# Turning the row maxima of an attention kernel with products in PV's form, and sending them in eight pieces

## The chip, the core and the metric

One core of a Trainium2 chip runs the whole program. Its engines work side by side, each from a queue of its own: TensorE (PE; its weight loads are PEld), VectorE (DVE), ScalarE (ACT), GpSimd (POOL) and SyncE (SP, which here issues nearly all DMAs). The metric is the device time of one execution in microseconds. The comparison is of medians of several runs.

## What is computed

An adaLN block: layer norm with shift and scale, attention with 32 query heads and one key and value head, a second layer norm, a bilinear GLU. The change touches the attention, more exactly the maximum that its softmax takes off the scores.

```python
S, D, H = 2048, 512, 32              # Dh = D // H = 16, F = 1792
h = layernorm(x) * (1 + ca) + sa     # sa, ca, ga, sb, cb, gb from silu(c) @ w_mod
q = (h @ wq) by heads; k = h @ wk; v = h @ wv     # one k and v for all heads
scores = einsum("bhqd,bkd->bhqk", q, k) * Dh ** -0.5
p = softmax(scores)                  # over 2048 keys
x = x + ga * (einsum("bhqk,bkd->bhqd", p, v) by heads @ wo)
h = layernorm(x) * (1 + cb) + sb
x = x + gb * (((h @ w_gate) * (h @ w_up)) @ w_down)
```

## The kernel before, in words

The attention is cut into 32 units of 256 queries and 8 heads. A unit has 16 steps over blocks of 128 keys. The scores are made twice. A first pass (`max_mm`, line 601) makes them with queries on the partitions, and VectorE takes the maximum of each row of 512 keys (line 605). A second pass (`qk_exp`, lines 657 and 659) makes them with keys on the partitions, ScalarE takes their exponential into a tile P (line 661), and `pv` (line 670) multiplies P by V. The first pass runs ahead of the second by LEAD steps, so that the maxima of unit u + 1 are complete some six steps before the second pass comes to it.

The maximum reaches the second pass as two more rows of its contraction. The query tile `sst[u % 3]` has 48 rows per half with the query in split f16, and rows 48 and 49 of each half (partitions 48, 49, 112 and 113) with the maximum divided by 32, split in two f16 parts; the key tile `kst` has -32 in the same rows. That is why the first pass reads 48 rows and the second 50. The maxima lie on 128 partitions by 16 columns (queries by blocks), and have to be turned before they can lie along a row. `max_fin` (line 622) takes the last maximum; `max_rows` gives back two functions: `f` turns the maxima on TensorE, and `g` splits them on ScalarE (line 634, the high part) and VectorE (line 635, the rest) and has SP send both to the rows of `sst` (line 639).

The code is written in the order in which each engine is to run it (`manual_schedule`); there is no scheduler behind it. `max_half` puts `f` and `g` aside for the next step. `late_max` calls `f` from `end_turn`, as a rule right behind `pv`, and `g` goes to `posts`, which are issued at the next opportunity. One unit's `pv` works in four products at a time, each of 32 columns of V, into four blocks of 32 partitions. Products of 64 rows in two halves (line 511, the projections and the GLU, and lines 601 and 659) stand around it.

In the first units SP also brings slices of the GLU weights into `hfs`, f32 slots in the tile `kwb`, for GpSimd to square and sum over rows (lines 944 and 946) into `ssqs`, which lie in the same tile: slots 4 to 7.5 and 8 to 11.5. The slots that the slices use are named in `SLOTS` (line 35). `kng`, half a slot behind slot 11, is read by the first unit's first pass alone.

Of the kernel before, what the change touches and what calls it, by code (L numbers as in the profile page):

```python
# [13 lines left out]
F32 = mybir.dt.float32  # L14
F16 = mybir.dt.float16
# [7 lines left out]
BT = S // NB  # L23
# [8 lines left out]
SQ_GAP = 2.6  # L32
LAG = 2
ROW_LAG = 4
SLOTS = (0, 1, 2, 3, 6, 7)
SUM_GAP = 4.0
SUM_LAG = 3
SPLIT_GAP = 2.5
# [25 lines left out]
def adaln_mqa_glu_kernel(ctx: ExitStack, tc: tile.TileContext, x_in, wq_in, wk_in, wv_in, wo_in,  # L64
                         wg_in, wu_in, wd_in, c_in, wm_in, out):
    nc = tc.nc
# [3 lines left out]
    consts = ctx.enter_context(tc.tile_pool(name="consts", bufs=1))  # L70
    big = ctx.enter_context(tc.tile_pool(name="big", bufs=1))
    work = ctx.enter_context(tc.tile_pool(name="work", bufs=2))
# [7 lines left out]
    def ps_hold(name="side", shape=(128, 512)):  # L80

        tag, bufs = pool.popleft()
        t = psum.tile(list(shape), F32, name=name, tag=tag, bufs=bufs)
        held[id(t)] = (t, tag, bufs)
        return t

    def ps_give(t):
        _, tag, bufs = held.pop(id(t))
        pool.append((tag, bufs))
# [47 lines left out]
    ident = consts.tile([128, 128], F32, name="ident")  # L137
# [8 lines left out]
    for i in range(3):  # L146
        t = consts.tile([128, 2, 2, ST], F16, name=f"sst{i}")
# [76 lines left out]
    kwb = big.tile([128, 2 * FT * D], F16, name="kwb", tag="wd")  # L224
    hfs = kwb[:, 0:2 * NHF * BT].bitcast(F32).rearrange("p (n t) -> p n t", n=NHF)
    ssqs = [kwb[:, 2 * n * BT:2 * n * BT + 2 * F].bitcast(F32) for n in (KC, 2 * KC)]
    kng = kwb[:, 2 * NHF * BT:2 * NHF * BT + BT]

    def hf(b, k):
# [107 lines left out]
    for k in range(KC):  # L337
        for j in range(4):
            nc.tensor.matmul(pmA[32 * j:32 * j + 32, 0:256], silr[:, k, 0:32], wmA[:, k, 256 * j:256 * j + 256],
                             start=(k == 0), stop=(k == KC - 1))  # L340
# [275 lines left out]
        relus.clear()  # L616

    mms = {}

    def max_fin(u):  # L620
        mms[u] = work.tile([128, 2, 8], F32, name="mm")
        nc.vector.tensor_reduce(mms[u], mparts[u], axis=AX.X, op=OP.max)

    def max_rows(u):
        def f():
            mms[u, "b"] = ps_hold("mxt")
            p = mms[u, "b"][0:16, 0:128]
            mms[u, "p"] = p
            nc.tensor.transpose(p, mms[u].rearrange("p a c -> p (a c)"), ident)  # L629

        def g():
            p = mms[u, "p"]
            mt = [work.tile([16, 128], F16, name=f"mt{hl}") for hl in range(2)]
            nc.scalar.activation(mt[0], p, AF.Copy, scale=1.0 / 32.0)
            nc.vector.scalar_tensor_tensor(mt[1], p, 1.0 / 32.0, mt[0], op0=OP.mult, op1=OP.subtract)
            ps_give(mms[u, "b"])
            s = sst[u % 3]
            for hl in range(2):
                nc.sync.dma_start(s[48 + hl:113 + hl:64].rearrange("p c q n -> p (c q n)"), mt[hl])
        return [(100, f, g)]  # L640

    pvb = {}
# [250 lines left out]
    def late_weights():  # L893
# [35 lines left out]
        taken = [0]  # L929

        def stage(n):
            if "d" in W:
                t = work.tile([128, D], F32, name="wsl", tag="xl", bufs=3)
            else:
                t = hfs[:, SLOTS[taken[0] % len(SLOTS)], :]
                taken[0] += 1
            nc.sync.dma_start(t[:, :sl[n][3]], sl[n][2])
            st[n] = t
# [24 lines left out]
        def norms(order):  # L963
            ns = [n for m in order for n in range(len(sl)) if sl[n][0] == m]
            out = []
            waiting = deque()
            for j in range(len(ns) + LAG):
                q = j - LAG

                def f(j=j, q=q):  # L970
                    if j < len(ns):
                        stage(ns[j])
                    if q >= 0:
                        square(ns[q])
                out.append((SQ_GAP, nothing, f))
                if waiting and j >= waiting[0][0]:
                    out.append((0,) + sums(*waiting.popleft()[1:]))
                if q >= 0 and (q == len(ns) - 1 or sl[ns[q]][0] != sl[ns[q + 1]][0]):
                    waiting.extend((j + SUM_LAG, sl[ns[q]][0], n) for n in range(4))
            out.append((SUM_GAP, nothing, nothing))  # L980
            return out + [(2,) + sums(*w[1:]) for w in waiting]

        def row_norms(ns):
            out = []
            for j in range(len(ns) + ROW_LAG):
                def f(j=j):
                    if j < len(ns):
                        stage(ns[j])
                    if j >= ROW_LAG:
                        t, n = st[ns[j - ROW_LAG]], j - ROW_LAG  # L990
                        nc.scalar.activation(t, t, AF.Square, accum_out=rown[:, n:n + 1])
                out.append((0, nothing, f))
            return out
# [66 lines left out]
        def split(n):  # L1060
            m, (i, c), v, w = sl[n]

            def load():
                if m < 2 and "g" not in W:
                    W["g"] = big.tile([128, 2, KC, F], F16, name="wg", tag="wg")
                    W["u"] = big.tile([128, 2, KC, F], F16, name="wu", tag="wu")
                elif m == 2 and i == 0:
                    W["d"] = big.tile([128, 2, FT, D], F16, name="wd", tag="wd")
                stage(n)

            def gate():
                if m >= 2:
                    nc.gpsimd.tensor_tensor(st[n], st[n], gbb if m == 2 else gab, op=OP.mult)

            def halves():
                t = st[n][:, :w]
                wt = wo if m == 3 else W["gud"[m]]
                if m < 2:
                    nc.gpsimd.tensor_scalar(t, t, sca[:, m:m + 1], 0.0, op0=OP.mult, op1=OP.add)
                nc.gpsimd.tensor_scalar(wt[:, 0, i, c], t, 1.0, 0.0, op0=OP.mult, op1=OP.add)  # L1080
                nc.gpsimd.tensor_tensor(wt[:, 1, i, c], t, wt[:, 0, i, c], op=OP.subtract)
            return load, gate, halves
# [45 lines left out]
    def max_half(a):  # L1128
        n = mstep[a]
        mstep[a] += 1  # L1130
        if n >= len(flat):
            return
        u, i, last, ops = flat[n]
        max_parts(u)
        for kind, p, t, kc in ops[a]:
            max_mm(u, a, (kind, p, t, kc))
        if mstep[1 - a] <= n:
            return
        u, i, last, ops = flat[n]
        if 0 < u < NU - 1 and i == QPRE:  # L1140
            load_q(u + 1)
        if i == 12:
            max_parts(u + 1)
        if last:
            max_fin(u)
            (_, f, g), = max_rows(u)
            later[min(mstep) + 1] = (f, g)
# [164 lines left out]
    u = NU - 1  # L1312
# [64 lines left out]
```

## Time and profile before

| | us |
|---|---|
| median of 3 runs | 1664.51 (1664.37 to 1664.66) |
| the profiled execution: span | 1663.8 |
| TensorE busy | 1643.3 (99%) |
| VectorE busy | 1402.3 (84%) |
| ScalarE busy | 1234.8 (74%) |
| GpSimd busy | 523.5 (31%) |
| TensorE's share of the chain that ended last | 93% |

The profile is of one execution. An engine's busy time is a union of its instructions; TensorE's products overlap in the records, so that the distance between their starts tells what one costs, not its duration. A row of the timeline joins instructions of the same kind that follow one another (x8 is eight), with the start in us from the beginning of the span, and behind it the duration of the whole. A q behind an engine's name (SPq, PEldq) is its sequencer, which waits and issues.

### The profile page before, as it was taken

Reading aid. Unit: us, or ns where it says so; the run is one execution under the profiler, and the core shown is the slowest. Engines: PE = TensorE matmul, PEld = TensorE weight load, DVE = VectorE, ACT = ScalarE, POOL = GpSimd, SP = SyncE. Lnnn points to the kernel's source line nnn. Section 1 sums busy time; section 2 is a strip of 40 time slices with the busy share of each in tenths; the row PEclk is TensorE's granted clock in tenths of the full one; section 3 lists DMA queues with packets and bytes.
Section 4 is the critical chain, followed back from the end, with each engine's and each line's share of the span. In section 5 each row is a group of like instructions: output and inputs, shape, how many; then the busy total and the mean of one; then the engine's idle time right before and its main releaser. Section 6 shows DMA issues by size and latency. Waiting matters only on the chain.

```text
span 1663.8 us, 39821 instructions
## 1 busy us (share of the span) xinstructions
PE 1643.3 (99%) x15677; PEld 747.1 (45%) x15677; DVE 1402.3 (84%) x2434; ACT 1234.8 (74%) x2389; POOL 523.5 (31%) x833
## 2 busy tenths in 40 slices
PE   8899999999999999999999999999999999999999
PEld 4333333355533554335543355434545345454776
DVE  7999999998998999899998999999998999980211
ACT  5688888888777877777877787777878777877300
POOL 4857537864841111301112011300113001210322
PEclk9999999999999999999999999999999999999999
DMA  6313313342210001000000000000000000000100
GB/s 237 108 59 100 95 43 120 96 129 80 77 51 24 18 12 32 19 32 20 20 26 23 25 13 24 26 25 26 20 29 15 26 22 20 26 14 21 33 13 14
DMA packets 66024, 75.39 MB, mean 45 GB/s; under 512 B 17702, under 2 KB 46634, under 8 KB 65836
## 3 DMA queue, kind: packets, MB, share of 16 engines
q1 hardware_dynamic: 63724, 72.26, 13.7%
q8 instruction: 123, 2.02, 0.5%
q10 hardware_dynamic: 2112, 0.59, 0.1%
q14 instruction: 65, 0.53, 0.1%
HBM read 55.51 MB, written 17.04 MB: 44 GB/s over the span
## 4 chain that ended last, share of the span: by engine, by line
PE 93%; ACT 2%; DVE 2%; DMA 1%; issue 1%; POOL 0%; SPq 0%; ACTq 0%; DVEq 0%
PE side L511 41%; PE pv L670 30%; PE mx L601 8%; PE sc L659 8%; PE sc L657 3%; ACT P L661 2%; DVE mpart L605 1%; DMA xbig<-in_A_x_dram 1%; PE mx L805 1%; PE mxt L629 0%; ACT hf L813 0%; PE sc L601 0%; DVE bs L248 0%; DMA kwb<-in_B_w_down_dram 0%; DMA wkv<-in_A_wv_dram 0%
## 5 line engine op out<-in xcount | busy, mean ns | idle before, releaser
L605 DVE TENSOR_REDUCE mpart<-mx 128x1 f32<-128x512 f32 x2016 | 1274.1, 684 | 104.0 <-PE mx L601 95.7
L661 ACT ACTIVATE P<-sc 128x512 f32<-128x512 f32 x2048 | 1094.8, 598 | 274.2 <-PE sc L659 226.9
L601 PE MATMUL mx<-kst,sst 48*128 48x512 f16 x2032 | 631.5, 377 | 3.8 <-ACT P L661 1.7
L659 PE MATMUL sc<-sst,kst 50*128 50x512 f16 x1792 | 597.5, 379 | 0.6 <-ACT P L661 0.3
L670 PE MATMUL pv<-P,vst 128*32 128x512 f32 x4096 | 545.3, 605 | 0.7
L511 PE MATMUL side<-h2T,wg 64*128 64x256 f16 (+1 forms) x2396 | 540.8, 271 | 0.1
L511 PE MATMUL side<-h2T,wu 64*128 64x256 f16 (+1 forms) x2396 | 538.7, 270 | 0.0
L511 PEld LDWEIGHTS <-wg 64*128 64x128 f16 (+1 forms) x2396 | 226.0, 94 | 230.5 <-ACT P L661 194.0
L511 PE MATMUL side<-wd,glu 64*128 64x512 f16 (+1 forms) x1172 | 272.8, 378 | 0.2 <-ACT P L661 0.2
L850 POOL TENSOR_SCALAR glu<-gf 128x256 f16<-128x256 f32 x112 | 45.8, 409 | 671.3 <-DVE gf L849 583.9
L511 PEld LDWEIGHTS <-wu 64*128 64x128 f16 (+1 forms) x2396 | 226.4, 94 | 43.0 <-issue 7.8
L601 PEld LDWEIGHTS <-sst 48*128 48x128 f16 x2064 | 189.9, 94 | 34.2 <-issue 17.4
L659 PEld LDWEIGHTS <-kst 50*128 50x128 f16 x1792 | 162.9, 94 | 63.0 <-issue 50.3
L511 PEld LDWEIGHTS <-glu 64*128 64x128 f16 (+1 forms) x1172 | 98.5, 94 | 192.4 <-ACT P L661 85.9
L670 PEld LDWEIGHTS pv<-P,vst 128*32 128x32 f32 x4096 | 80.7, 108 | 160.9 <-issue 150.1
L849 DVE TENSOR_TENSOR gf<-side,g 128x256 f32<-128x256 f32 x112 | 46.7, 418 | 79.8 <-ACT g L847 77.7
L657 PE MATMUL sc<-sst,kst 50*128 50x256 f16 x512 | 96.9, 268 | 0.1
L511 PE MATMUL side<-h,wq 64*128 64x512 f16 (+1 forms) x372 | 95.0, 376 | 0.4 <-ACT P L661 0.4
L847 ACT ACTIVATE g<-side 128x256 f32<-128x256 f32 x112 | 42.3, 379 | 65.6 <-PE side L511 65.3
L511 PE MATMUL side<-wo,och 64*128 64x512 f16 (+1 forms) x360 | 86.3, 377 | 0.0
L851 POOL TENSOR_TENSOR glu<-gf,glu 128x256 f16<-128x256 f32 x112 | 75.3, 673 | 9.3
L706 POOL TENSOR_TENSOR oc<-oc,rr 128x256 f32<-128x256 f32 x31 | 22.7, 731 | 146.6 <-DMA rr<-ri 100.4
(233 smaller groups left out, 865.4 us busy)
## 6 DMA issues: line engine op xcount, KB each, us to landing
pd<-ev SPq DMA_DIRECT2D x32, 256.0 KB
kwb<-in_B_w_gate_dram SPq DMA_DIRECT2D x32, 224.0 KB
kwb<-in_B_w_up_dram SPq DMA_DIRECT2D x32, 224.0 KB
sst<-qd SPq DMA_DIRECT2D x180, 32.0 KB
qd<-q SPq DMA_DIRECT2D x16, 256.0 KB
oc<-pd SPq DMA_DIRECT2D x64, 64.0 KB
rr<-ri SPq DMA_DIRECT2D x64, 64.0 KB
x<-in_A_x_dram SPq DMA_DIRECT2D x14, 256.0 KB
```

Of the source, the lines that this page charges most:

```text
L511: return nc.tensor.matmul(self.p[:, c * w:(c + 1) * w], left[rows], right[rows], start=start and c == 0, stop=stop and c == len(terms) - 1)
L601: nc.tensor.matmul(m, s[64 * a:64 * a + 48, t // 2, p, t % 2 * 128:(t % 2 + 1) * 128], w[64 * a:64 * a + 48, :], start=(i == 0), stop=(i = ...
L605: nc.vector.tensor_reduce(part, m, axis=AX.X, op=OP.max)
L657: nc.tensor.matmul(t[:, c * ST:(c + 1) * ST], keys, s[64 * a:64 * a + 50, c, p, :], start=True, stop=True)
L659: nc.tensor.matmul(t.rearrange("k (c n) -> k c n", c=2), keys, s[64 * a:64 * a + 50, :, p, :], start=True, stop=True)
L661: ex = nc.scalar.activation(ptl[u, kt, p, a], t, AF.Exp)
L670: nc.tensor.matmul(pvb[u][32 * j:32 * j + 32, :], vst[:, kt, :], ptl[u, kt, p, a], start=(kt == 0), stop=(kt == KT - 1))
L706: eng.tensor_tensor(o, o, st["r"], op=OP.mult)
L847: nc.scalar.activation(g, p[:, 0:ST], AF.Copy, scale=2.0 ** -45)
L849: nc.vector.tensor_tensor(gf, p[:, ST:2 * ST], g, op=OP.mult)
L850: nc.gpsimd.tensor_scalar(glu()[:, 0, f, :], gf, 1.0, 0.0, op0=OP.mult, op1=OP.add)
L851: nc.gpsimd.tensor_tensor(glu()[:, 1, f, :], gf, glu()[:, 0, f, :], op=OP.subtract)
```

## The change

The maxima go to a fixed tile `mmc`, 32 columns wide for each of two units in turn, of which 16 are used and 16 stay zero. Instead of one transpose of 128x16, `f` makes four f32 products whose stationary operand is this 128x32 tile and whose moving operand is a block of 32 columns of the identity; each goes to 32 partitions of PSUM of its own, as the four products of `pv` do. The turned maxima then lie on 128 partitions by 32 columns (16 of every 32 partitions count) instead of 16 by 128, and each of the two f16 parts goes to `sst` in four transfers, each from sixteen rows. The last two slots of the weight slices move from 6 and 7 to 12 and 13, behind the squares.

```diff
-SLOTS = (0, 1, 2, 3, 6, 7)
+SLOTS = (0, 1, 2, 3, 12, 13)
...
+    stg = kwb.bitcast(F32).rearrange("p (n t) -> p n t", t=BT)
...
+    mmc = consts.tile([128, 2, 32], F32, name="mmc")
+    nc.gpsimd.memset(mmc, 0.0)
 
     def max_fin(u):
-        mms[u] = work.tile([128, 2, 8], F32, name="mm")
+        mms[u] = mmc[:, u % 2, 0:16].rearrange("p (a c) -> p a c", a=2)
         nc.vector.tensor_reduce(mms[u], mparts[u], axis=AX.X, op=OP.max)
 
     def max_rows(u):
         def f():
             mms[u, "b"] = ps_hold("mxt")
-            p = mms[u, "b"][0:16, 0:128]
+            p = mms[u, "b"][:, 0:32]
             mms[u, "p"] = p
-            nc.tensor.transpose(p, mms[u].rearrange("p a c -> p (a c)"), ident)
+            for j in range(4):
+                nc.tensor.matmul(p[32 * j:32 * j + 32, :], mmc[:, u % 2], ident[:, 32 * j:32 * j + 32], start=True, stop=True)
 
         def g():
             p = mms[u, "p"]
-            mt = [work.tile([16, 128], F16, name=f"mt{hl}") for hl in range(2)]
+            mt = [work.tile([128, 32], F16, name=f"mt{hl}") for hl in range(2)]
...
             for hl in range(2):
-                nc.sync.dma_start(s[48 + hl:113 + hl:64].rearrange("p c q n -> p (c q n)"), mt[hl])
+                to = s[48 + hl:113 + hl:64].rearrange("p c q (h j n) -> p j (c q h) n", h=2, j=4)
+                for j in range(4):
+                    nc.sync.dma_start(to[:, j], mt[hl][32 * j:32 * j + 16, :])
...
-                t = hfs[:, SLOTS[taken[0] % len(SLOTS)], :]
+                t = stg[:, SLOTS[taken[0] % len(SLOTS)], :]
```

In the program the change shows on three queues. On TensorE near the end of unit 5, where the maxima of unit 6 are turned; before (line 670 is PV, 511 a side product of the GLU, 659 the scores):

```order
2907 L670 MATMUL pv<-P,vst 32x512 x3
2908 L670 MATMUL pv<-P,vst 32x512 [waits Activation_49]
2909 L629 MATMUL mxt<-ident,mm 16x128 [waits DVE_49,PE_49]
2910 L511 LDWEIGHTS wg [waits Activation_49]
2911 L511 MATMUL side<-h2T,wg 128x256 [waits Pool_49]
```

The same place in the changed program, where the lines count six more:

```order
2911 L676 MATMUL pv<-P,vst 32x512 x3
2912 L676 MATMUL pv<-P,vst 32x512 [waits Activation_49]
2913 L633 MATMUL mxt<-ident,mmc 32x32 [waits DVE_49,PE_49]
2914 L633 MATMUL mxt<-ident,mmc 32x32 x3
2915 L512 LDWEIGHTS wg [waits Activation_49]
2916 L512 MATMUL side<-h2T,wg 128x256 [waits Pool_49]
```

Four products stand where the transpose stood, with its waits and its neighbours. On SP, where the rows are sent behind that (mt is the split maximum, DMAHW names the eight counters that DMAs are waited for by); before:

```order
182 L937 DMA kwb<-in_B_w_gate_dram 128x448 [waits DMAHW2_49,Pool_49]
183 L639 DMA sst_128<-mt_5130 2x8x128 [waits DMAHW3_49,Activation_49]
184 L639 DMA sst_128<-mt_5131 2x8x128 [waits DMAHW4_49,DVE_49]
185 L937 DMA kwb<-in_B_w_gate_dram 128x448 [waits DMAHW5_49,Pool_49]
186 L937 DMA kwb<-in_B_w_down_dram 128x512 [waits DMAHW6_49,Pool_49]
```

And in the changed program:

```order
219 L645 DMA sst_128<-mt_5182 2x8x32 [waits DMAHW7_49,Activation_49]
220 L645 DMA sst_128<-mt_5182 2x8x32 [waits DMAHW0_49]
221 L645 DMA sst_128<-mt_5182 2x8x32 [waits DMAHW1_49]
222 L645 DMA sst_128<-mt_5182 2x8x32 [waits DMAHW2_49]
223 L645 DMA sst_128<-mt_5183 2x8x32 [waits DMAHW3_49,DVE_49]
224 L645 DMA sst_128<-mt_5183 2x8x32 [waits DMAHW4_49]
225 L645 DMA sst_128<-mt_5183 2x8x32 [waits DMAHW5_49]
226 L645 DMA sst_128<-mt_5183 2x8x32 [waits DMAHW6_49]
227 L943 DMA kwb<-in_B_w_gate_dram 128x448 [waits DMAHW7_49,Pool_49]
228 L943 DMA kwb<-in_B_w_down_dram 128x512 [waits DMAHW0_49,Pool_49]
```

Eight transfers stand in the place of two, the weight slices behind them, and the eight take all eight counters. On TensorE where unit 6 begins and its first scores read the rows; before:

```order
2993 L670 MATMUL pv<-P,vst 32x512 x4
2994 L511 LDWEIGHTS wg [waits Activation_49]
2995 L511 MATMUL side<-h2T,wg 128x256
2996 L659 LDWEIGHTS kst [waits DMAHW4_49,DMAHW3_49]
2997 L659 MATMUL sc<-sst_128,kst 128x512 [waits PE_49]
```

And in the changed program:

```order
2998 L676 MATMUL pv<-P,vst 32x512 x4
2999 L512 LDWEIGHTS wg [waits Activation_49]
3000 L512 MATMUL side<-h2T,wg 128x256
3001 L665 LDWEIGHTS kst [waits DMAHW4_49,DMAHW5_49,DMAHW3_49,DMAHW6_49,DMAHW2_49,DMAHW7_49,DMAHW1_49,DMAHW0_49]
3002 L665 MATMUL sc<-sst_128,kst 128x512 [waits PE_49]
```

The order is the same; the weight load of the first scores waits for all eight counters instead of two.

## Rows read from the trace of the kernel before

**Rows 1.** The page: span, TensorE's busy time, the chain that ended last.

```profile
span 1663.8 us, 39821 instructions
PE 1643.3 (99%) x15677; PEld 747.1 (45%) x15677; DVE 1402.3 (84%) x2434; ACT 1234.8 (74%) x2389; POOL 523.5 (31%) x833
...
PE 93%; ACT 2%; DVE 2%; DMA 1%; issue 1%; POOL 0%; SPq 0%; ACTq 0%; DVEq 0%
```

**Rows 2.** Busy time by stretch; then who VectorE's maxima (line 605) wait for, 500:1500.

```profile
core 0: us, PE busy (x) PEld busy (x) DVE busy (x) ACT busy (x) POOL busy (x), PEclk, DMA share, GB/s
...
500.00:1000.00 500.00, 499.48 (x5061) 227.51 (x5059) 457.93 (x770) 393.51 (x754) 83.15 (x149) 1.00 0.07 22
1000.00:1500.00 500.00, 499.26 (x5073) 227.84 (x5069) 457.07 (x770) 393.24 (x755) 87.20 (x161) 1.00 0.07 22
...
  PE mx L601: 76.1, 229
```

**Rows 3.** Timeline of TensorE, end of unit 5: start, duration, engine, line, operation, count.

```profile
327.51 1.06 PE L670 MATMUL pv<-P,vst 128*32 128x512 f32 x8
328.51 0.28 PE L629 MATMUL mxt<-ident,mm 128*16 128x128 f32 x1
328.72 0.28 PE L511 MATMUL side<-h2T,wg 64*128 64x256 f16 x1
```

**Rows 4.** Timeline of TensorE in unit 0, products of line 956 behind PV.

```profile
112.57 1.06 PE L670 MATMUL pv<-P,vst 128*32 128x512 f32 x8
113.45 0.40 PE L956 MATMUL mx<-kwb,onec 128*32 128x128 f32 x8
113.78 0.39 PE L659 MATMUL sc<-sst,kst 50*128 50x512 f16 x1
```

**Rows 5.** Timeline of SP, rows for units 2, 6 and 14; a pair in unit 16.

```profile
154.81 1.20 SPq L639 DMA_DIRECT2D sst<-mt  x2
...
329.11 1.19 SPq L639 DMA_DIRECT2D sst<-mt  x2
...
707.62 1.19 SPq L639 DMA_DIRECT2D sst<-mt  x2
...
824.72 1.10 SPq L700 DMA_DIRECT2D rr<-ri  x2
```

**Rows 6.** Issues by line: ns min/median/max; then six of line 566 in the timeline.

```profile
L639 SPq DMA_DIRECT2D sst<-mt x64: 508/542/659, 68.9 to 1500.8; - x64
...
L700 SPq DMA_DIRECT2D rr<-ri x64: 507/526/545, 137.6 to 1563.1; - x64
...
825.91 2.75 SPq L566 DMA_DIRECT2D sst<-qd  x6
```

**Rows 7.** Timeline of SP, from the rows for unit 30 on.

```profile
1453.92 1.19 SPq L639 DMA_DIRECT2D sst<-mt  x2
1465.70 0.34 SPq L679 DMA_DIRECT2D pd<-ev  x1
1467.71 0.57 SPq L686 DMA_DIRECT2D rc<-pd  x1
1468.38 1.09 SPq L690 DMA_DIRECT2D oc<-pd  x2
1478.19 0.34 SPq L695 DMA_DIRECT2D ri<-rc  x1
1479.94 1.09 SPq L700 DMA_DIRECT2D rr<-ri  x2
```

**Rows 8.** Busy time and DMA share (last but one) behind the issues at 1453.92.

```profile
1455.10:1455.20 0.10, 0.10 (x6) 0.05 (x2) 0.10 (x1) 0.10 (x1) 0.00 (x0) 1.00 0.14 33
...
1455.30:1455.70 0.40, 0.40 (x8) 0.16 (x8) 0.40 (x2) 0.37 (x2) 0.00 (x0) 1.00 0.00 0
...
1455.80:1455.95 0.15, 0.15 (x8) 0.00 (x0) 0.15 (x1) 0.15 (x1) 0.00 (x0) 1.00 0.09 19
1455.95:1456.20 0.25, 0.25 (x8) 0.00 (x0) 0.25 (x2) 0.25 (x2) 0.00 (x0) 1.00 0.00 0
```

**Rows 9.** Timeline of TensorE's weight loads: first scores of units 2, 6 and 14.

```profile
159.54 0.09 PEld L659 LDWEIGHTS <-kst 50*128 50x128 f16 x1 [0.84 <-issue]
...
334.46 0.09 PEld L659 LDWEIGHTS <-kst 50*128 50x128 f16 x1
...
712.11 0.09 PEld L659 LDWEIGHTS <-kst 50*128 50x128 f16 x1
```

**Rows 10.** Timeline of ScalarE behind the transpose for unit 6.

```profile
328.82 0.27 ACT L634 ACTIVATE mt<-mxt 16x128 f16<-16x128 f32 x1 [0.54 <-PE mxt L629]
329.20 2.12 ACT L661 ACTIVATE P<-sc 128x512 f32<-128x512 f32 x4
```

**Rows 11.** TensorE's second wait ahead of the transpose: ns min/median/max.

```profile
L629 PEldq EVENT_SEMAPHORE  x31: 51/51/51, 68.2 to 1452.4; - x31
```

**Rows 12.** Timeline: a weight load that waited for ScalarE's P.

```profile
331.55 0.09 PEld L511 LDWEIGHTS <-wg 64*128 64x128 f16 x1 [0.84 <-ACT P L661]
```

**Rows 13.** TensorE's waits for GpSimd's squares: us in total, times, longest.

```profile
PE mx L956 <- POOL kwb L946: 1.6, 1, 1.6
```

## The prediction

> **What bounds the kernel now.** I read the page first [rows 1]: TensorE is busy for 99% of a span of 1663.8 us, and 93% of the chain that ended last is its own. Then the stretches [rows 2]: from 500 to 1500 us it has under 1.5 us of idle time in 1000, at full granted clock, while VectorE is busy for 915 us and ScalarE for 787. So in the 32 units whatever shortens TensorE's stream shortens the kernel, and whatever stops that stream is added in full: nothing behind it could win the time back. The reader should see in the rows of VectorE's waits that its maxima still wait for TensorE 229 times in this stretch [rows 2]; it is close to full, but it follows.
>
> The path that the change touches is one per unit: the transpose of the maxima on TensorE, two short splits on ScalarE and VectorE, transfers issued by SP, and then the first score product of the next unit, which needs the rows that they bring. It is short work, so I looked at two distances: what the transpose holds of TensorE, and how long before their use the rows arrive.
>
> **What the turning costs.** For unit 6, at the end of unit 5, two sets of four P times V products start at 327.51, the transpose at 328.51, the next products at 328.72 [rows 3]: 1.21 us from the first PV product to the next work. The products of the form that the new ones copy are in the kernel already: line 956, 128x32 in f32, behind the same two sets. There they begin 0.88 us after the first PV product, and two sets of 128 columns hold the engine for 0.33 us until the next work [rows 4]. So staying in PV's form saves 0.12 us ahead of the products (1.00 against 0.88), and the switch is then paid once, behind them. Two sets of 512 columns took 0.88 us, 0.44 each; in proportion a set of 128 takes 0.11, and of the 0.33 us for two such sets and the switch 0.11 is left for the switch. One set of 32 columns is then 0.03 us, with the switch 0.14, with 0.02 for issuing four products instead of one 0.16: the new way takes 0.88 + 0.16 = 1.04 us against 1.21. I take 0.16 us saved; the ends are 0 (the one set costs as much as both sets there) and 0.22 (only the switch remains). Over 32 units that is 5.1 us of gain (0 to 7).
>
> **What the sending costs.** SP issued two transfers per unit, and 1.19 us were enough for both. Eight now stand in a row in its queue, one behind the other. The price of an issue: two of line 639 take 1.19 us, each with two waits; pairs with one wait take 1.09 and 1.10 us (lines 690 and 700) [rows 5 to 7]. The cheapest issues are those of line 566, six in 2.75 us, 0.47 a step [rows 6]. The new transfers have the shape of the old ones with shorter runs (two partitions by eight runs, out of sixteen partitions), so I take the dear kind: six steps of 0.57 (1.10 less line 700's median issue of 0.53) and one of 0.66, where the first transfer of the second half has two waits. The eighth issue begins 6 x 0.57 + 0.66 = 4.08 us after the first; the ends are 3.3 (0.47 a step) and 4.6 (0.66 a step).
>
> From the beginning of an issue to its landing no row gives the SBUF-to-SBUF time directly. In unit 30 the packets of the two transfers move 1.2 to 1.3 and 1.8 to 2.0 us after the first issue, so the second's data are there 1.3 us after its own beginning [rows 7, 8]; waiters are released 1.75 us after the issue of ri and 2.01 us after that of pd [rows 7], which both go to DRAM. I take 1.65, with ends 1.3 and 2.0. Last landing: 4.08 + 1.65 = 5.73 us after the first issue, where it was 0.66 + 1.65 = 2.31.
>
> The first score product of the next unit loads its weights at 334.46 in unit 6, 5.35 us after the first issue at 329.11 [rows 5, 9]. Up to now the rows were there some 3 us ahead, and nobody waited. Both ends of this distance move. The turning ends earlier: 0.12 us for the start, the rest from shorter splits (ScalarE's took 0.27 us over 128 columns [rows 10], now 32); I take 0.20 for the first issue, ends 0.10 and 0.26. The product becomes due earlier too, by the 0.16 us saved: 5.19 us after the old first issue.
>
> The weights load also has a new set of waits: eight DMA queues instead of two. A second wait costs TensorE's sequencer a 51 ns instruction of its own [rows 11], and the queues are waited for in a fixed order, whichever landed last; by the program's order some three remain behind the last landing on average, 0.15 us. From the end of a wait to the load it released I take 0.23 us: ScalarE's P tiles end at 331.32, the load that waited for them starts at 331.55 [rows 10, 12].
>
> So the load can start at 5.73 + 0.15 + 0.23 - 0.20 = 5.91 us, and is due at 5.19: TensorE stands for **0.72 us**. I count 25 units like unit 6. In units 1 to 3 the product comes earlier, in unit 2 4.73 us after the first issue [rows 5, 9]; with that for all three each loses 1.34 us, 4.0 together. In unit 14 it comes after 4.49 us [rows 5, 9], which gives 1.6. In units 0, 4 and 10 other work stands before it, it comes after the rows, and nothing is lost. Sum: 25 x 0.72 + 4.0 + 1.6 = 23.6 us lost, 5.1 gained, 18.5 to the worse.
>
> By the Trainium skill, "DMA: Bandwidth & Descriptors", Issuing engines are not separate DMA queues, the time that a sequencer takes to initiate a DMA is usually small beside the DMA itself. Here the issue of line 639 has a median of 0.54 us [rows 6], a third of the way to the landing, so the rows speak against it; if it held for the new transfers, the sum would be the gain alone, the time of the first rival below.
>
> **The rest costs nothing that I can price.** The two splits get shorter and stay hidden: ScalarE waited 0.54 us for the transpose [rows 10]. Their extra waits, for transfers of two units before, are passed in that idle time. The maxima now lie in one fixed tile, used in turn by even and odd units, which is as deep as the two buffers before; its clearing is one GpSimd instruction at the start. SP's other transfers behind the eight start 3.4 us later: weight slices in the first units and rows of x later, which are asked for several steps ahead; if that cover were gone, GpSimd's weight work and then TensorE would wait. Of the new slots, two weight slices no longer land on columns of the accumulated squares. That takes a wait away from SP and GpSimd, neither of which is on the path; the only place where TensorE waits for the squares is one of 1.6 us [rows 13], so at best 1.6 us is gained. I count 0.
>
> **Rivals.** *The rows come in time and only the gain is left.* If an issue costs what line 566's costs, the eighth begins at 3.3 + 0.05 us and lands at 3.35 + 1.65 = 5.0, or 4.8 with the earlier start, and the load could go at 5.03: ahead of 5.19. Then the whole gain stays: 1664.5 - 5 = 1659.5, faster. For it: SP has done six in 2.75 us. Against it: those have another shape, and the shape that is kept never took under 0.51 us.
>
> *The rows come in time, but the waits are in the way.* Six more waits of 51 ns stand on TensorE's sequencer right ahead of the load, 0.31 us, of which the end of the PV products covers some. 0.15 to 0.2 us a unit eats the 5.1 us: 1660 to 1667, no change.
>
> *The whole queue is slow.* If each issue takes 0.66 us or the landing 2.0, a unit loses 0.4 to 0.5 us more: 1693 to 1699 (29 units), and with both some 1709.
>
> *The change doesn't do what it says:* the small products switch the array's form after all. Then the 5.1 us are missing, and the forecast's mechanism gives 1688.
>
> **How the numbers follow.** The profiled execution's span is 0.7 us under the median of the runs, 1664.5; I add the difference to the median: 1664.5 + 18.5 = 1683.0. Chances: the wait for the late rows, in the sizes from 1668 to 1702, 0.70 (with the case without the gain in it); slower still 0.06; waits in the way of rows that are in time 0.14; the gain alone 0.10. A difference of 0.2%, 3.3 us, is about what can be told from no change here: faster 0.10, same 0.14, slower 0.76. The range leaves out the slowest case and the pure gain: 1660 to 1700.
>
> **What would show it.** In the profile after: the first score product of a unit, or the side product beside it, waits for a DMA (the tile sst from mt) in some 29 units, 0.5 to 1.3 us each; TensorE's idle time in the stretch from 500 to 1500 us rises from 1.3 to some 17 us; eight issues stand in a row in SP's timeline and take 4.6 us; from the first PV product to the work behind the turned maxima 1.05 us instead of 1.21. I am wrong if that row of issues takes under 4 us, if the data land in under 1.3 us, or if the products behind PV don't start at 0.88 us.

## The result and the profile after

The changed kernel takes 1671.72 us (median; 1670.99 to 1672.88) against 1664.59 for the one before: a ratio of 1.004, 95% interval 1.0028 to 1.0051. It is slower by 7.1 us, not by the forecast 18.5. One of its six executions took 3600 us, for a reason that no run here shows: the range and the ratio leave it out, and without it the median is 1671.47.

The page of the changed kernel: span, busy time, the chain that ended last, and the score products of line 665 (busy us, mean ns of one | idle time ahead of them, and what ended most of it); last, from the view of the waits, how long those products waited for the transfers of the rows (us in total, times, longest).

```profile
span 1669.7 us, 40589 instructions
...
PE 1644.7 (99%) x15901; PEld 756.8 (45%) x15901; DVE 1397.8 (84%) x2434; ACT 1232.3 (74%) x2389; POOL 525.1 (31%) x834
...
PE 89%; DVE 5%; ACT 3%; DMA 1%; issue 1%; SPq 1%; POOL 0%; ACTq 0%; DVEq 0%
...
L665 PE MATMUL sc<-sst,kst 50*128 50x512 f16 x1792 | 597.1, 378 | 6.7 <-DMA sst<-mt 4.2
...
PE sc L665 <- DMA sst<-mt: 4.2, 6, 0.8
```

Against [rows 1] the span is 5.9 us longer with TensorE as busy as before. What is new is in the last two lines: score products now wait for the transfers of the rows, and SP has a place in the chain (SPq, 1%). The waits are few: 4.2 us in 6 of them, where the prediction wanted some 29 of 0.5 to 1.3 us.

TensorE at the end of unit 5 (start us, duration, line, operation, count of records), the place of [rows 3]:

```profile
329.38 1.06 PE L676 MATMUL pv<-P,vst 128*32 128x512 f32 x8
330.27 0.24 PE L633 MATMUL mxt<-ident,mmc 128*32 128x32 f32 x8
330.44 0.28 PE L512 MATMUL side<-h2T,wg 64*128 64x256 f16 x1
```

The turned maxima start 0.89 us after PV and the next work 1.06 us after PV, instead of 1.00 and 1.21. In ns from the last PV product to the next work: 733 before, 586 after, 147 saved in each of 30 units. The gain is there.

TensorE's weight loads where unit 20 begins, of the kernel before and then of the changed one (what stands in brackets is idle time ahead of a load and its releaser):

```profile
991.03 0.09 PEld L511 LDWEIGHTS <-wg 64*128 64x128 f16 x1 [0.84 <-ACT P L661]
991.03 0.09 PEld L659 LDWEIGHTS <-kst 50*128 50x128 f16 x1
```

```profile
995.20 0.09 PEld L512 LDWEIGHTS <-wg 64*128 64x128 f16 x1 [0.84 <-ACT P L667]
995.47 0.09 PEld L665 LDWEIGHTS <-kst 50*128 50x128 f16 x1 [0.17 <-issue]
```

Before, the first scores' load went out with the side product's. Now it comes 0.27 us behind it, and that is where the time goes. The line's other rows in that stretch show what the sequencer did in between (count: ns min/median/max, first and last start):

```profile
L665 PEldq EVENT_SEMAPHORE  x4: 51/51/61, 995.0 to 995.4; - x4
```

Four waiting instructions stand ahead of this load where there was one. The first takes one counter and the others two each; the load takes the eighth itself. They start 5.748, 5.859, 5.965 and 6.111 us after the first turning product, the load 6.186. The last row landed at 5.991. A record of 51 ns does not by itself say that nothing was waited for: in unit 2 all four have 51 ns, though they stand 0.48 to 0.54 us apart, and the last three each start 0.03 us after a landing. The distances have to be read too. Here the third instruction lasted 61 ns and the fourth stands 0.146 us behind it instead of 0.107, so some 0.04 us was waited for the last row; the rest of the gap is the instructions themselves.

TensorE's idle time hides this. In the two stretches of [rows 2]:

```profile
500.00:1000.00 500.00, 498.13 (x5105) 229.29 (x5103) 454.43 (x768) 390.32 (x751) 83.23 (x150) 1.00 0.07 22
1000.00:1500.00 500.00, 498.88 (x5144) 231.74 (x5142) 457.07 (x772) 391.77 (x754) 87.76 (x162) 1.00 0.08 23
```

It rises from 1.3 to 3.0 us only, though the changed kernel falls 3.5 us further behind between units 10 and 31, after a gain of 147 ns in nearly every one. The recorded ends of PV's products (0.59 us each) lie over a gap of 0.3 us. The gap shows between the starts.

**Where the 7 us are.** For every unit I compared the distance from the first turning product to the first scores' load with that of before. *Due* is the load's time before, moved by the shorter turning. *Waits* is what the chain of waiting instructions adds if none has to wait: from the first one's start, 107 ns for each further one and 76 to the load, less due; a first instruction that comes late itself is in it. (In units 1, 19 and 23 a late row comes in on the first counter and holds that instruction. Against its start with six transfers that is some 0.7 of the changed kernel's 6.4 us.) *Late* is the rest, up to the load's real start. The split takes the chain first; without it, late rows alone would have held many of the same loads. The control is the kernel before, for LEAD 32 with the same LEAD. Units 1 to 31, in us:

| kernel | turning | waits | late | sum | measured against its control |
|---|---|---|---|---|---|
| changed | -4.4 | +6.4 | +7.0 | +8.9 | +7.1 |
| old transpose, eight transfers | 0 | +6.4 | +5.9 | +12.2 | +12.1 |
| one product, two transfers | -0.3 | 0 | 0 | -0.3 | -1.2 |
| two products, four transfers | -3.3 | +0.6 | +0.2 | -2.5 | -4.9 |
| three products, six transfers | -3.1 | +2.6 | +0.1 | -0.4 | -1.7 |
| changed, LEAD 32 | -0.3 | +9.1 | +2.8 | +11.7 | +11.2 |

The experiments behind the lines come next. The 9.1 us of the last line hold one stall of 3.8. The measured times lie 0.1 to 2.4 us under the sums. With LEAD at 30 the larger part of this is a wait that the table does not reach, since it ends at the first scores' load. In units 6 and 7 of the kernel before, ScalarE waits for slices of w_down to square, so P comes late and TensorE waits for P. In the changed kernel, and in the next four lines of the table, this is gone but for 0.2 us. Waits in the kernel before, then in the changed one:

```profile
ACT kwb L991 <- DMA kwb<-in_B_w_down_dram: 2.1, 2, 1.2
PE mx L601 <- ACT P L661: 1.7, 3, 0.9
```

```profile
PE mx L602 <- ACT P L667: 0.2, 1, 0.2
```

From the first scores' load to the next turning, the changed kernel's units 6 and 7 are 1.1 and 1.3 us shorter than before, the others mostly 0.1 to 0.3, of which 0.11 is the earlier turning that the table has. Some 2 us less bring the sums of the changed kernel and of two products within 0.4 us of the measured ones, and two more within 1.0; that of the old transpose then lies some 2 too low, which stays open. It is not the new slots: the wait is gone with the old ones too.

*Late* in the changed kernel is no matter of all units: 2.3 us in units 1 to 3, 1.9 in units 6 to 8, 0.9 in unit 14, 1.9 in all the rest.

The next view shows two of those units, the first scores' loads of units 2 and 6 in the changed kernel:

```profile
160.84 0.09 PEld L665 LDWEIGHTS <-kst 50*128 50x128 f16 x1 [1.69 <-DMA sst<-mt]
...
337.09 0.09 PEld L665 LDWEIGHTS <-kst 50*128 50x128 f16 x1 [0.81 <-issue]
```

In unit 2 the scores are due 5.40 us after the turning, and the rows land at 6.24. In unit 6 they land at 6.61 instead of 5.99; from 300 to 500 us the DMA engines' share is 0.29, from 500 on 0.07.

### The profile page after: what moved, and what is told of

It reads as the page before. It is cut to its first block, busy times and chain, and to the rows that moved or that the text cites. A ratio compares the mean times of both kernels' runs of the same rounds, so it can differ in the third digit from the quotient of the medians.

```text
span 1669.7 us, 40589 instructions
## 1 busy us (share of the span) xinstructions
PE 1644.7 (99%) x15901; PEld 756.8 (45%) x15901; DVE 1397.8 (84%) x2434; ACT 1232.3 (74%) x2389; POOL 525.1 (31%) x834
## 4 chain that ended last, share of the span: by engine, by line
PE 89%; DVE 5%; ACT 3%; DMA 1%; issue 1%; SPq 1%; POOL 0%; ACTq 0%; DVEq 0%
PE side L512 39%; PE pv L676 28%; PE mx L602 9%; PE sc L665 8%; DVE mpart L606 4%; PE sc L663 3%; ACT P L667 2%; DMA sst<-mt 1%; DMA xbig<-in_A_x_dram 1%; PE mx L811 1%; SPq L645 1%; ACT hf L819 0%; PE sc L602 0%; DVE bs L249 0%; DMA wkv<-in_A_wv_dram 0%
```

## The experiments

Three theories. **A**, the prediction's: eight transfers in a row bring the rows too late. **B**: the four waiting instructions hold TensorE even when the rows are there. **C**: the small products cost what the transfers were blamed for. Diffs are against the changed kernel. Kernels that are compared ran on one chip beside the kernel before (1665.5 or 1665.6 us there). The expectations reckon with a saving of 0.176 us a unit, 5.6 in all; that is the distance from the first of the four products to the next work. What the traces show as saved is 0.147, 4.4 in all.

### The old transpose with eight transfers

```diff
-            p = mms[u, "b"][:, 0:32]
+            p = mms[u, "b"][0:16, 0:128]
...
-                nc.tensor.matmul(p[32 * j:32 * j + 32, :], mmc[:, u % 2], ident[:, 32 * j:32 * j + 32], start=True, stop=True)
+            nc.tensor.transpose(p, mms[u].rearrange("p a c -> p (a c)"), ident)
...
-                    nc.sync.dma_start(to[:, j], mt[hl][32 * j:32 * j + 16, :])
+                    nc.sync.dma_start(to[:, j], mt[hl][:, 32 * j:32 * j + 32])
```

This is the kernel before with the sending alone changed; what the cut does not show, the slots among it, is as before.

> The old transpose to 16x128, but each half sent in four pieces of 32 columns: the sending alone. Theory A (rows that land late hold TensorE at the first scores) and theory B (TensorE's sequencer passes the waits for eight counters in four instructions 0.11 us apart, which cost even when the rows are in time) both say: all of the loss without the gain, 1664.6 + 7.1 + 5.6 (32 x 0.176 us, the saving in the two traces) = 1677. Theory C (the four small products themselves hold TensorE, not the sending): the time of before, 1664.6.

1677.56 us, ratio 1.007 (1.0058 to 1.0083): 12.1 us slower. C falls: the whole loss comes with the transfers, and the new products win back 5 of it. Where unit 20 begins, the same gap stands behind the side product, 0.32 us:

```profile
999.21 0.09 PEld L511 LDWEIGHTS <-wg 64*128 64x128 f16 x1 [0.84 <-ACT P L663]
999.53 0.09 PEld L661 LDWEIGHTS <-kst 50*128 50x128 f16 x1 [0.23 <-issue]
```

### One product of 128 columns with the old two transfers

```diff
...
-            for j in range(4):
-                nc.tensor.matmul(p[32 * j:32 * j + 32, :], mmc[:, u % 2], ident[:, 32 * j:32 * j + 32], start=True, stop=True)
+            nc.tensor.matmul(p, mmc[:, u % 2], ident, start=True, stop=True)
...
-                to = s[48 + hl:113 + hl:64].rearrange("p c q (h j n) -> p j (c q h) n", h=2, j=4)
-                for j in range(4):
-                    nc.sync.dma_start(to[:, j], mt[hl][32 * j:32 * j + 16, :])
+                nc.sync.dma_start(s[48 + hl:113 + hl:64].rearrange("p c q n -> p (c q n)"), mt[hl])
```

> One product in PV's form with all 128 columns of the identity, 32 stationary columns of which 16 are zero: the maxima lie on 16 rows by 128 as before, and two transfers send them as before. The form without the sending. From line 956's set of 128 columns it holds TensorE 0.41 + 0.21 us from the last PV product to the next work, 0.11 less than the transpose's 0.73: A and B say 1664.6 - 3.6 = 1661. C says no gain: 1664.6 or above.

1664.30 us, ratio 0.9992 (0.9983 to 1.0000): 1.2 us under the kernel before, hardly clear of noise, where 3.6 were expected. The timeline of TensorE at the beginning of unit 20's turning says why:

```profile
981.83 1.06 PE L673 MATMUL pv<-P,vst 128*32 128x512 f32 x8
982.71 0.38 PE L632 MATMUL mxt<-ident,mmc 128*32 128x128 f32 x2
983.03 0.28 PE L512 MATMUL side<-h2T,wg 64*128 64x256 f16 x1
```

One product shows as two records, 110 ns apart, and the old transpose as one [rows 3]. So 724 ns pass from the last PV product to the next work, against 733: staying in PV's form wins 114 ns ahead of it and the second record takes them back behind it.

### Two products of 64 columns with four transfers

```diff
-            p = mms[u, "b"][:, 0:32]
+            p = mms[u, "b"][0:64, 0:64]
...
-            for j in range(4):
-                nc.tensor.matmul(p[32 * j:32 * j + 32, :], mmc[:, u % 2], ident[:, 32 * j:32 * j + 32], start=True, stop=True)
+            for j in range(2):
+                nc.tensor.matmul(p[32 * j:32 * j + 32, :], mmc[:, u % 2], ident[:, 64 * j:64 * j + 64], start=True, stop=True)
...
-            mt = [work.tile([128, 32], F16, name=f"mt{hl}") for hl in range(2)]
+            mt = [work.tile([64, 64], F16, name=f"mt{hl}") for hl in range(2)]
...
-                to = s[48 + hl:113 + hl:64].rearrange("p c q (h j n) -> p j (c q h) n", h=2, j=4)
-                for j in range(4):
+                to = s[48 + hl:113 + hl:64].rearrange("p c q (h j n) -> p j (c q h) n", h=2, j=2)
+                for j in range(2):
```

> Two products of 64 columns of the identity into two blocks of 32 partitions, four transfers. The turning costs 0.03 us more than with four blocks (gain 4.7 us). The last of four landings comes over 2 us ahead of its use. A: only the gain is left, 1659.9. B: four counters take two instructions instead of one, 0.1 us in 29 units: 1662.5.

**1660.59 us, ratio 0.9973 (0.9963 to 0.9984): faster than both kernels**, 4.9 us under the one before. The 109 ns saved make 3.3 of it in 30 units; most of the rest is the wait of units 6 and 7, which is gone. The turning takes 624 ns, 109 saved; the rows land 3.9 us after it; two waiting instructions are left, and the gap at unit 20 is 0.02 us:

```profile
988.37 0.09 PEld L512 LDWEIGHTS <-wg 64*128 64x128 f16 x1 [0.84 <-ACT P L667]
988.39 0.09 PEld L665 LDWEIGHTS <-kst 50*128 50x128 f16 x1
```

### Three products of 64 columns with six transfers

```diff
...
-            for j in range(4):
-                nc.tensor.matmul(p[32 * j:32 * j + 32, :], mmc[:, u % 2], ident[:, 32 * j:32 * j + 32], start=True, stop=True)
+            for j, c in enumerate((0, 32, 64)):
+                nc.tensor.matmul(p[32 * j:32 * j + 32, :], mmc[:, u % 2], ident[:, c:c + 64], start=True, stop=True)
...
-                for j in range(4):
-                    nc.sync.dma_start(to[:, j], mt[hl][32 * j:32 * j + 16, :])
+                wide = s[48 + hl:113 + hl:64].rearrange("p c q (h j n) -> p j (c q h) n", h=2, j=2)
+                for j, t in enumerate((to[:, 0], to[:, 1], wide[:, 1])):
+                    nc.sync.dma_start(t, mt[hl][32 * j:32 * j + 16, 0:t.shape[-1]])
```

> Three products of 64 columns (the first two are sent in their first 32 columns alone), six transfers. The last landing is about 4.9 us behind the turning, 0.9 ahead of its use. A: 1659.9. B: six counters take three instructions, 0.2 us in 29 units: 1665.7.

1663.81 us, ratio 0.9987 (0.9978 to 0.9996): 1.7 us faster, between the two. In unit 20 the rows land 4.98 us after the turning, 0.9 us before the load is due, so A leaves nothing to lose. It is so in all 25 units that the prediction counted as alike: the rows have landed at least 0.66 us before the first waiting instruction, and in 23 of them the load still comes 0.04 to 0.19 us after its due time. Three waiting instructions stand there in unit 20, 0.11 us apart and none longer than 51 ns, and the load comes 0.12 us behind the side product's:

```profile
L666 PEldq EVENT_SEMAPHORE  x3: 51/51/51, 989.6 to 989.9; - x3
```

```profile
989.81 0.09 PEld L512 LDWEIGHTS <-wg 64*128 64x128 f16 x1 [0.84 <-ACT P L668]
989.93 0.09 PEld L666 LDWEIGHTS <-kst 50*128 50x128 f16 x1
```

One, two, three and four such instructions leave a gap of 0, 0.02, 0.12 and 0.27 us. The first extra one is nearly free, since the sequencer had 0.10 us to spare before; each further one costs 0.10 us; the last step of 0.15 has the 0.04 of the late row in it. This is B in the rows, if cheaper than in its 1665.7. The time alone would not decide: the turning takes 630 ns here and saves 103, so that A without any loss would stand at 1662.3, or some 2 us lower with the wait of units 6 and 7 gone.

### LEAD 31: the rows were to come earlier

The constant that sets how far the first pass runs ahead was raised, in the kernel before, the changed one and the one with two products.

```diff
-LEAD = 30
+LEAD = 31
```

> The kernel before with LEAD at 31 instead of 30: the first pass runs one step further ahead, so the rows are sent some 1.4 us earlier against their use. They were in time already, so neither theory sees a change of over 2 us from 1664.6. It is the control of the next run.

> The changed kernel with LEAD at 31: all eight transfers have landed about 1 us before the first scores are due. Theory A (late rows hold TensorE): only the gain of the products is left, 5.6 us under the control, some 1659. Theory B (the waits for eight counters, four instructions 0.11 us apart behind the side product, cost 0.3 us a unit though the rows are in time): 31 x 0.3 - 5.6 = 4 us above the control, some 1668.

> Two products of 64 columns and four transfers with LEAD at 31. A and B: as with LEAD at 30, 4 to 5 us under the control, some 1660, since the rows were in time there by 2 us already.

1668.23, 1673.51 and 1664.96 us; ratios to the kernel before 1.0016 (1.0007 to 1.0025), 1.0050 (1.0037 to 1.0062) and 0.9998 (0.9989 to 1.0006). Against the control that is +5.3 and -3.3 us, much as without the edit. The control itself is 2.7 us above the kernel before, more than the 2 expected; why is not shown. The trace shows that the edit did not do what it was for: for unit 5 and all later ones the turning comes behind the same PV, and in unit 20 the rows land at 5.98 us with due times as before. It says nothing on A against B.

### The old slots

```diff
-SLOTS = (0, 1, 2, 3, 12, 13)
+SLOTS = (0, 1, 2, 3, 6, 7)
```

> The changed kernel with the old SLOTS (0, 1, 2, 3, 6, 7). If the slots cost or gain nothing, as predicted: 1671.7. At most the one wait of 1.6 us comes back: 1673.3.

1670.68 us, ratio 1.0036 (1.0023 to 1.0048), against 1.0040 (1.0028 to 1.0051) for the change as a whole. The slots make no difference that can be measured.

### LEAD 32: the rows are there

```diff
-LEAD = 30
+LEAD = 32
```

> The kernel before with the constant LEAD at 32 in place of 30, the control of the next two. Unlike LEAD at 31, by the order of the program this sets the turning one PV earlier in the units from the fourth on, so that one more PV stands between it and the scores that wait for the rows. No theory is at stake: the three units of start-up move too. Within 10 us of 1665.

> The changed kernel with LEAD at 32: the eight transfers land at the same 6.0 us after the turning, but the first scores fall due about 1 us or more later, so that in the units from the fourth on the rows are there before TensorE's sequencer comes to the waits. Theory A (rows that land late hold TensorE): only the cheaper turning is left, 5.6 us under its control or close to it. Theory B (the four instructions that wait for eight counters cost 0.3 us a unit even when the rows are there): 30 x 0.3 - 5.6, 3 to 4 us over its control.

> Two products of 64 columns and four transfers with LEAD at 32. Rows that landed 3.9 us after the turning were in time already at LEAD 30, so both theories expect what that kernel gained there over its control: about 5 us under the control with LEAD at 32. A further gain would say that its rows were late as well.

1672.68 us for the kernel before (ratio 1.0040, 1.0026 to 1.0053), 1683.91 for the changed one (1.0111, 1.0097 to 1.0124), 1675.43 for two products (1.0055, 1.0043 to 1.0068). The changed kernel is 11.2 us over its control. A's figure, 5.6 under, is out, and B's 3 to 4 over is far too small. Nor do the rows land 6.0 us after the turning: from unit 6 on it is 7.4 to 8.0 (9.2 in unit 14), since the first issue begins 2.0 to 2.5 us after it instead of 0.54 (3.7 in unit 14). Three things are in the 11.2, and the trace takes them apart.

First, B itself. In 23 of the units from 6 on, all but 7, 10 and 14, nothing is waited for: the four instructions follow one another at 0.105 to 0.111 us (0.14 in four of 69 cases), and *late* is at most 0.03 us. In 15 of the 23 the last row had landed 0.13 to 0.37 us before the first of the four, and the load still comes 0.15 to 0.28 us after its due time, 3.2 us in these 15. Unit 30 is one of them: the last row lands at 7.75 us after the turning, the first instruction starts at 8.08, and the load comes at 8.47 instead of 8.24. The loads in the control, then the waiting instructions and the loads in the changed kernel:

```profile
1466.88 0.09 PEld L511 LDWEIGHTS <-wg 64*128 64x128 f16 x1 [0.84 <-ACT P L661]
1466.89 0.09 PEld L659 LDWEIGHTS <-kst 50*128 50x128 f16 x1
```

```profile
L665 PEldq EVENT_SEMAPHORE  x4: 51/51/51, 1476.6 to 1476.9; - x4
```

```profile
1476.75 0.09 PEld L512 LDWEIGHTS <-wg 64*128 64x128 f16 x1 [0.84 <-ACT P L667]
1476.97 0.09 PEld L665 LDWEIGHTS <-kst 50*128 50x128 f16 x1
```

Second, the gain is gone. With LEAD at 32 a side product or a score product and not PV stands ahead of the turning, here in unit 20 of the control and of the changed kernel:

```profile
989.66 0.27 PE L511 MATMUL side<-h2T,wu 64*128 64x256 f16 x1
989.86 0.28 PE L629 MATMUL mxt<-ident,mm 128*16 128x128 f32 x1
990.07 0.28 PE L511 MATMUL side<-h2T,wg 64*128 64x256 f16 x1
```

```profile
996.87 0.27 PE L512 MATMUL side<-h2T,wu 64*128 64x256 f16 x1
997.07 0.27 PE L633 MATMUL mxt<-ident,mmc 128*32 128x32 f32 x8
997.27 0.28 PE L512 MATMUL side<-h2T,wg 64*128 64x256 f16 x1
```

From the product ahead to the next work it is 409 ns with the transpose and 400 with the four products. In these runs the 147 ns of the change are won behind PV and nowhere else. That is also why two products win nothing here (+2.7 us; the intervals overlap). The Trainium skill, "TensorEngine Tiling (Array Packing)", Key Properties, says that a change of tiling mode drains TensorE. The trace is in line with it, with 523 ns from PV to the transpose against 409 to products of PV's form, but no row shows the drain itself.

Third, a single stall of 3.8 us in unit 7, on queues that neither theory spoke of. Waits there, 375 to 395 us (in total, times, longest), and SP's timeline:

```profile
ACT kwb L997 <- DMA kwb<-in_B_w_down_dram: 4.1, 1, 4.1
PE mx L602 <- ACT P L667: 3.9, 1, 3.9
```

```profile
379.89 4.45 SPq L645 DMA_DIRECT2D sst<-mt  x8
384.39 0.40 SPq L943 DMA_DIRECT2D kwb<-in_B_w_down_dram  x1
```

The slice of w_down stands behind the eight transfers, ScalarE's squaring waits for it (0.9 us in the control, where two transfers stand ahead of it), P waits for ScalarE, and TensorE for P. This is the cover that the prediction counted on for SP's other transfers, though it looked for the wait on GpSimd and not on ScalarE. It holds in the changed kernel, where TensorE waits 0.2 us for P; here it is gone, once.

## Why the prediction was wrong in size

**The gain: right.** Forecast 0.16 us a unit, measured 0.147; the way there was partly luck. A product in f32 shows as two records (32 units by 16 steps by 4 products of PV are 2048, and the page counts 4096), so what I read as two sets of PV, and as two sets in [rows 4], was one set with two records for each product. The four new products also have two records each. 0.33 us less 0.11 for the switch is 0.22 for two rounds of 128 columns, 0.055 for two of 32, with the switch 0.17; measured are 0.176 from the first of the four to the next work.

**The mechanism: right in kind, in part.** The first scores are held by the eight transfers, at the load that was named, but not by late rows alone: the chain of waiting instructions costs by itself (see the rivals). The step that failed is the term of 0.72 us a unit that TensorE stands. In its own frame, from the first issue of before, for unit 20:

| step | forecast | measured |
|---|---|---|
| eighth issue after the first | 4.08 | 3.94 (0.56 a step) |
| landing after its issue | 1.65 | 1.51 |
| first issue earlier by | 0.20 | 0.18 (0.12 from PV, 0.06 from shorter splits) |
| from the last landing to the load | 0.15 + 0.23 | 0.195 |
| the load can start at | 5.91 | 5.47 |
| it is due at | 5.19 | 5.15 |
| TensorE stands | **0.72** | **0.32** |

No single step is off by more than 0.19 us, and those that had ends lie inside them. But the term is the difference of two numbers above 5, and three errors of 0.14, 0.14 and 0.19 point the same way: more than half of it goes. In the 25 units together the table's *waits* and *late* come to 9.5 us, 0.38 a unit, where 18.0 were forecast: 8.5 of the 11.4 us of the miss. Units 1 to 3 and 14 make 1.8 more, the wait for P that went away in units 6 and 7 about 2, and the gain that was 0.7 smaller takes some off again. The step that missed most is the one from landing to load: I put a chain of waits *behind* the last landing. In the trace most of that chain runs while the last rows are still on their way, and its last instruction starts 0.12 us after the last landing. That differs from unit to unit, since the counters are waited for in a fixed order and the last row comes in on another of them each time: from the last landing to the load it is 0.04 us in unit 13, and 0.43 in units 19 and 23, where the whole chain stands behind it; the mean of the 25 is 0.20.

The signs of being wrong that I had set say nothing of this. All three steps are on the right side of them: landing 1.51 us, products 0.89 us behind PV, and the row of issues in unit 20:

```profile
989.82 4.43 SPq L645 DMA_DIRECT2D sst<-mt  x8
```

**The other units.** Units 1 to 3 lose 2.6 us together instead of 4.0, unit 14 1.2 instead of 1.6. In units 6 to 8 the rows land 0.6 to 0.75 us later than elsewhere, which I had not forecast: I gave these units the landing of a quiet queue.

**The rivals.** *Waits in the way* was the better half of the story, and I gave it 0.14. I priced six instructions of 51 ns. There are three more than before, since one takes up to two counters, and they follow one another at 0.107 us; 0.32 us less 0.09 to 0.17 of cover comes to 0.15 to 0.23, against the 0.15 to 0.28 measured. Its time of 1660 to 1667 was too low because the rows are not in time everywhere. With the changed kernel alone the two causes cannot be told apart in an ordinary unit: rows that land at 5.99 and a chain that ends at 6.1 to 6.2 both lie past a load that is due at 5.87 to 5.95. Six transfers, and LEAD at 32 in the 15 units where the rows come early, show that the chain costs by itself; unit 2 and units 6 to 8 show that late rows do. *Only the gain is left* and *the whole queue is slow* did not come: a step took 0.56 us and neither 0.47 nor 0.66. *The products switch the form after all* did not come either: they start 0.89 us behind PV.

**The edits at nothing.** The slots are nothing, and TensorE's wait of 1.6 us for the squares is still there. SP's later start of other transfers cost TensorE nothing in the changed kernel, and 3.8 us once where its cover was gone. What the prediction did not look at are the waits for P behind ScalarE's squares, 1.7 us before and 0.2 after.

**Left open.** Why ScalarE no longer waits for w_down in units 6 and 7 of the changed kernels; the 2 us by which the sum of the old transpose is off once that is counted; and why LEAD at 32 makes the kernel before 7 us slower.

## What to carry to other kernels

- Count what the consumer has to wait for, not only when the data land. Splitting two transfers into eight added three waiting instructions ahead of one weight load, some 0.2 us a unit, more than the 0.147 that the better products had won; with four transfers the first extra instruction was free and the gain stayed.
- A loss that is the difference of two long paths needs its own range. Ends of 3.3 to 4.6 us on one step against a slack of 5.2 allow both signs of the result, and the middle of each step does not make the middle of the loss.
- A cheaper form of a product is worth what stands next to it. The same four products saved 147 ns behind PV and 9 ns behind a side product.

## What the runs showed of the hardware that I had not expected

- Eight counters cost TensorE's sequencer four waiting instructions of 51 ns (one counter, then two, two and two; the load takes the last), and these follow one another at 0.105 to 0.111 us when nothing has to be waited for.
- An issue on SP took 0.50 us (median) for 2x8x32, 0.52 for 2x8x64 and 0.54 for 2x8x128 elements: a quarter of the data saved 8% of the issue.
- A product in f32 against a block of the identity goes in two records 0.11 us apart at 128 columns, while the transpose of as many columns is one record.
